# A Mamba-2 scan with a bilinear feed-forward on one core: blocks of all four batches at once, with four tokens a partition and 32-row tiles

## The chip, the cores and the metric

The kernel runs on one core of a Trainium2 chip. The metric is the device time of one execution in microseconds (us). The span that a profile shows is 1.7 us shorter than the device time of the same run (138.7 against 140.43). Runs of one kernel scatter; each is marked fast or slow (slow: over 1.5% above the fastest of its kernel). The profiled run of the kernel before, 140.43 us, is a slow one, so its first microseconds may differ from those of a fast run.

## The reference

The first half is a scan over 768 positions for 4 batches and 8 heads, with head dimension 32 and state dimension 16. The second half multiplies its output, as 3072 tokens of 256 columns, by two matrices of 256 x 1536, multiplies the two results with each other, and multiplies that by a matrix of 1536 x 256.

```python
for c in range(nc):                        # chunks of 32 in the reference
    cum = np.cumsum(la, axis=-1)
    L = np.exp(cum[:, :, :, None] - cum[:, :, None, :]) * causal
    M = np.einsum('bhin,bhjn->bhij', Cc, Bc) * L
    y_intra = np.einsum('bhij,bhjd->bhid', M, xc)
    y_inter = np.einsum('bhin,bhnd->bhid', Cc, state) * decay_to_i[:, :, :, None]
    y[:, :, sl] = y_intra + y_inter
    state = decay_full[:, :, None, None] * state + np.sum(Bx, axis=2)
# ...
x = attn_out.transpose(0, 2, 1, 3).reshape(B * S, H * D)
out = ((x @ w_a) * (x @ w_b)) @ w_out
```

## The kernel before

The kernel uses blocks of 128 positions, six of them. A block's work has five parts on TensorE: the transposes of scaled B and C, the **scores** (B times C), the **values** (masked scores times x, on top of the product of C with the carried state, here called inter), the **state** product, and the feed-forward: **units** (two products of X with columns of the first two weights) and **output** products. Two batches are worked on at a time, a "pair". A partition holds two consecutive positions of one batch, so that a contraction over positions runs over 64 partitions twice.

```python
def scores(p):                             # p is a pair of batches in a block
    BT, CT = st[p]["BT"], st[p]["CT"]
    for e in range(2):
        for r in range(2):
            for m in range(4):
                for bt in range(2):
                    rows = slice(32 * m, 32 * m + 32)
                    c0 = (e * 2 + r) * Q
                    nc.tensor.matmul(
                        SC[m][64 * bt : 64 * bt + 64, c0 : c0 + Q],
                        BT[rows, e, r, bt], CT[rows, bt],
                        start=True, stop=True, skip_group_check=True,
                        tile_position=(32 * m, 64 * bt),
                    )
# ... the steady loop:
for p in range(4, NP):
    scores(p)
    if p + 1 < NP:
        scale(p + 1)                       # GpSimd: next C, B and x times their factors
    if p + 2 < NP:
        load(p + 2)                        # two pairs ahead
    h = unit(p - 1, 0)
    mask(p, 0)                             # VectorE: scores times the causal mask
    h()
    mask(p, 1)
    mask(p, 2)
    h = unit(p - 1, 1)
    h()
    mask(p, 3)
    go((p - 1, 2))
    out_half(p - 2, 0)
    go((p - 1, 3))
    pull(p)
    pv(p)                                  # inter, values, state product
    state(p)
    if p + 1 < NP:
        transposes(p + 1)
    out_half(p - 2, 1)
    # ... (fb)
    go((p - 1, 4), (p - 1, 5))
```

Of the kernel before, what the change touches and what calls it, by code (L numbers as in the profile page):

```python
# [22 lines left out]
def kernel(  # L23
# [17 lines left out]
    Q = 128  # L41
    NBLK = S // Q
# [3 lines left out]
    NQ = NK // 2  # L46
    BH = nb * H
    NBP = nb // 2
    NP = NBP * NBLK
# [19 lines left out]
    causal = const.tile([128, 2, Q], f16, name="causal")  # L69
    sel = const.tile([BH, 2, NBP, H], f32, name="sel")  # L70
# [11 lines left out]
    X2T = big.tile([128, NP, 2, 2, Q], f16, name="X2T")  # L82
    U32 = big.tile([128, NP, 2, 2 * D], f32, name="U32")
    gU = big.tile([128, NP, 2, 2 * D], f32, name="gU")
    maskbd = big.tile([128, H, D], f16, name="maskbd")
    warm = big.tile([128, 512], f16, name="warm")
    scr = big.tile([128, 8], f32, name="scr")
    Pr = big.tile([BH, NBLK, Q], f32, name="Pr")
    rmid = big.tile([BH, NBLK], f32, name="rmid")
    selr = big.tile([BH, NBLK, 2, NBP * H], f32, name="selr")  # L90
    fB = big.tile([128, NBLK, 2, NBP, H], f32, name="fB")
    fC = big.tile([128, NBLK, 2, NBP, H], f32, name="fC")
# [5 lines left out]
    inp = ctx.enter_context(tc.tile_pool(name="inp", bufs=3))  # L98
    mid = ctx.enter_context(tc.tile_pool(name="mid", bufs=3))
    ffh = ctx.enter_context(tc.tile_pool(name="ffh", bufs=4))  # L100
# [3 lines left out]
    SC0 = ps4.tile([128, 2, 512], f32, name="SC0")  # L104
    SC1 = ps4.tile([128, 2, 512], f32, name="SC1")
    SC = [SC0[:, 0], SC0[:, 1], SC1[:, 0], SC1[:, 1]]
    TT = SC0[:, 0, :].bitcast(f16)

# [3 lines left out]
    pair_in = {}  # L112

    def tiles(p):
        Bn = inp.tile([128, H, 2, N], f32, name="bn", tag="bn")
        Cn = inp.tile([128, H, 2, N], f32, name="cn", tag="cn")
        Xn = inp.tile([128, H, 2, D], f32, name="xn", tag="xn")
        pair_in[p] = (Bn, Cn, Xn)

    def load1(eng, p, which, bt):  # L120
        blk, bp = divmod(p, NBP)
        src = (B, C, x)[which][2 * bp + bt, :, blk * Q : (blk + 1) * Q, :]
        return eng.dma_start(
            pair_in[p][which][64 * bt : 64 * bt + 64].rearrange("i h r n -> i h (r n)"),
            src.rearrange("h (i r) n -> i h (r n)", r=2),
        )

    def load(p, eng=None):
        tiles(p)
        return [load1(eng or nc.sync, p, w, bt) for w in range(3) for bt in range(2)]  # L130
# [3 lines left out]
    tiles(1)  # L134
    load1(nc.scalar, 0, 1, 0)
    load1(nc.sync, 0, 0, 0)
    load1(nc.scalar, 0, 1, 1)
    load1(nc.sync, 0, 0, 1)
    nc.scalar.preload_act_table_set("natural_log_exp_and_others")
    nc.scalar.dma_start(c32, p32_t.ap())  # L140
    load1(nc.sync, 0, 2, 0)
    load1(nc.sync, 0, 2, 1)
    for bt in range(2):
        load1(nc.scalar, 1, 1, bt)
        load1(nc.sync, 1, 0, bt)
    load1(nc.sync, 1, 2, 0)
    load1(nc.scalar, 1, 2, 1)
# [9 lines left out]
        pattern=[[-H, 2], [-2 * H, NBP], [-1, H]],  # L157
# [10 lines left out]
    def load_w(q3):  # L168
        for W, src in ((Wa, moe_w_a), (Wb, moe_w_b)):
            c = slice(q3 * KC, (q3 + 1) * KC)  # L170
            wd.append(nc.gpsimd.dma_start(W[:, :, c], src.rearrange("(f p) e -> p f e", p=128)[:, :, c]))

    load_w(0)
    nc.gpsimd.memset(causal, 1.0)
    for bt in range(2):
        v = causal[64 * bt : 64 * bt + 64]
        nc.gpsimd.affine_select(
            out=v, in_=v, compare_op=ALU.is_ge, fill=0.0, base=0, pattern=[[-1, 2], [1, Q]], channel_multiplier=-2
        )

    def warmup(n):
        w = psf.tile([128, 512], f32, name="wps", tag="ff")
        for _ in range(n):
            nc.tensor.matmul(w[:, 0:128], warm[:, 0:128], warm[:, 0:128], start=True, stop=True, skip_group_check=True)  # L184
# [6 lines left out]
    def sel_over_mid(lo, hi):  # L191
        nc.vector.reciprocal(rmid[:, lo:hi], Pr[:, lo:hi, 63])
        nc.vector.tensor_tensor(
            out=selr[:, lo:hi].rearrange("p k t c -> p k (t c)"),
            in0=sel.rearrange("p t b h -> p (t b h)").unsqueeze(1).broadcast_to((BH, hi - lo, 2 * NBP * H)),
            in1=rmid[:, lo:hi].unsqueeze(2).broadcast_to((BH, hi - lo, 2 * NBP * H)),
            op=ALU.mult,
        )

    def factors_mm(lo, hi):  # L200
        fps = psf.tile([128, 512], f32, name="fps", tag="ff")
        F = fps[:, 0 : (hi - lo) * 2 * NBP * H].rearrange("p (k r c) -> p k r c", k=hi - lo, r=2)
        for k in range(lo, hi):
            for r in range(2):
                for bt in range(2):
                    nc.tensor.matmul(
                        F[64 * bt : 64 * bt + 64, k - lo, r],
                        Pr[:, k].rearrange("p (i r) -> p r i", r=2)[:, r],
                        selr[:, k, bt],
                        start=True,  # L210
                        stop=True,
                        skip_group_check=True,
                        tile_position=(0, 64 * bt),
                    )
        return F.rearrange("p k r c -> p (k r c)")

    def flat(f, lo, hi):
        return f[:, lo:hi].rearrange("p k r b h -> p (k r b h)")
# [4 lines left out]
    def scale_x(p, eng):  # L223
        X16 = mid.tile([128, H, 2, D], f16, name="x16", tag="x16")
        xo, xi = X16.rearrange("p h r d -> p (h r d)"), pair_in[p][2].rearrange("p h r d -> p (h r d)")
        st.setdefault(p, {})["X16"] = X16
        if eng is nc.scalar:
            nc.scalar.mul(xo, xi, XS)
        else:
            eng.tensor_scalar(xo, xi, XS, None, ALU.mult)  # L230

    def scale_bc(p, which, eng):
        blk, bp = divmod(p, NBP)
        name, f = (("bm", fB), ("cm", fC))[which]
        m_ = mid.tile([128, 2, H, N], f16, name=name, tag=name)
        eng.tensor_tensor(  # L236
            out=m_,
            in0=pair_in[p][which].rearrange("p h r n -> p r h n"),
            in1=f[:, blk, :, bp].unsqueeze(3).broadcast_to((128, 2, H, N)),
            op=ALU.mult,  # L240
        )
        st.setdefault(p, {})[name] = m_

    def scale(p):
        scale_bc(p, 1, nc.gpsimd)
        scale_bc(p, 0, nc.gpsimd)
        scale_x(p, nc.gpsimd)

    def transposes(p, ps=None):
        s = st[p]  # L250
        TB, TC = (TT[:, 0:256], TT[:, 256:512]) if ps is None else [t_.bitcast(f16)[:, 0:256] for t_ in ps]
        for T_, src in ((TB, s["bm"]), (TC, s["cm"])):
            for r in range(2):
                nc.tensor.transpose(  # L254
                    T_[:, r * 128 : (r + 1) * 128], src[:, r].rearrange("p h n -> p (h n)"), ident
                )
        BT = mid.tile([128, 2, 2, 2, 64], f16, name="bt", tag="bt")
        CT = mid.tile([128, 2, Q], f16, name="ct", tag="ct")
        for e in range(2):
            o_ = BT[:, e].rearrange("p r t i -> p (r t i)")  # L260
            nc.scalar.activation(out=o_, in_=TB, func=AF.Copy, scale=par[:, e : e + 1])  # L261
        (nc.scalar.copy if ps is None else nc.vector.tensor_copy)(  # L262
            CT.rearrange("p t (i r) -> p r (t i)", r=2), TC.rearrange("p (r c) -> p r c", r=2)
        )
        s["BT"], s["CT"] = BT, CT

    def scores(p):
        BT, CT = st[p]["BT"], st[p]["CT"]
        for e in range(2):
            for r in range(2):  # L270
                for m in range(4):
                    for bt in range(2):
                        rows = slice(32 * m, 32 * m + 32)
                        c0 = (e * 2 + r) * Q
                        nc.tensor.matmul(  # L275
                            SC[m][64 * bt : 64 * bt + 64, c0 : c0 + Q],
                            BT[rows, e, r, bt],
                            CT[rows, bt],
                            start=True,
                            stop=True,  # L280
                            skip_group_check=True,
                            tile_position=(32 * m, 64 * bt),
                        )
        st[p]["T1"] = mid.tile([128, H, 2, Q], f16, name="t1", tag="t1")

    def mask_on_pool(p, m):
        tmp = mid.tile([128, 2, 2 * Q], f32, name="tmp", tag="tmp")
        nc.scalar.copy(tmp.rearrange("p e c -> p (e c)"), SC[m])
        nc.gpsimd.tensor_tensor(
# [76 lines left out]
    def state(p):  # L366
        blk, bp = divmod(p, NBP)
        if blk == NBLK - 1:
            return
# [263 lines left out]
```

## Time and profile before

| | before |
|---|---|
| device time, median of 3 runs | 139.27 us (137.64 to 140.62) |
| span of the profiled run | 138.7 us (a slow run) |
| TensorE busy | 125.3 us, 90% |
| steady pair of batches, start to start | 9.38 us, so 18.76 us for a block of four batches |
| matmuls of TensorE in the profile, each with a weight load | 1977 |

In the lines below and in the prediction, a timeline row gives start, duration, engine, line, operation, output and inputs, tile, shapes and the number of instructions in the group; brackets give the idle time before it and what released it. Matmuls overlap their predecessors (twelve output matmuls from 81.14 us are 1.47 us long, and the next group starts 1.31 us behind their start), so costs are read from start to start. Of the names, cn, bn and xn are a block's C, B and x as loaded; cm and bm are C and B times their factors, and ct and bt the same transposed; t is a masked score, sbd the carried state spread out for inter, gU the carried state times its decay; X2T is the scan's output as the feed-forward reads it, aps and bps are a unit's two products, and hk is what they give when multiplied. One caution: the row of the granted clock of the kernel before reads 9 in all slices, and yet four feed-forward matmuls took 0.85 us instead of 0.44 until 23.5 us. The matmuls decide, not the row.

### The profile page before, as it was taken

The page shows a single profiled execution, that of the slowest core. Times are in us where ns is not written, and L with a number is a line of the kernel's source. Part 1 is how long each engine was busy: PE and PEld are TensorE (multiplying, and loading weights), DVE is VectorE, ACT ScalarE, POOL GpSimd, SP SyncE. Part 2 cuts the span into 40 slices and gives each one's busy share as a digit, 9 for nine tenths or more (in the row PEclk, how much of TensorE's full clock was granted, in tenths as well). Part 3 has the DMA queues.
Part 4 walks back from the last instruction along what each step waited for, and adds up shares of the span by engine and source line. Part 5 has one row for each costly group of instructions (what it writes and reads, how often), then busy time and mean ns, then how long its engine had stood idle before and what let it go on. Part 6 is the DMA issues. An engine that isn't in the chain of part 4 may idle for free.

```text
span 138.7 us, 4777 instructions
## 1 busy us (share of the span) xinstructions
PE 125.3 (90%) x1977; PEld 107.2 (77%) x1977; DVE 88.3 (64%) x166; ACT 73.3 (53%) x148; POOL 52.2 (38%) x71
## 2 busy tenths in 40 slices
PE   6993499799698699999999999999999999999990
PEld 6783366788597578988888888888888888888870
DVE  2681358678557649498497594894975937935340
ACT  3132253585267165754856647548556486465520
POOL 7947431595040665470740923805408200000000
PEclk9999999999999999999999999999999999999999
DMA  3999999500126635355145261451541011020112
GB/s 76 144 209 202 193 190 196 107 19 2 43 64 128 118 115 100 94 107 124 38 73 128 63 126 43 93 132 45 83 116 43 0 38 43 8 70 2 38 38 76
DMA packets 44805, 12.22 MB, mean 88 GB/s; under 512 B 38576, under 2 KB 44752, under 8 KB 44784
## 3 DMA queue, kind: packets, MB, share of 16 engines
q1 hardware_dynamic: 38736, 9.02, 31.3%
q0 software_dynamic: 3216, 2.36, 11.7%
q10 hardware_dynamic: 2832, 0.54, 2.3%
q8 instruction: 15, 0.25, 0.7%
q14 instruction: 6, 0.05, 0.1%
HBM read 11.13 MB, written 3.15 MB: 103 GB/s over the span
## 4 chain that ended last, share of the span: by engine, by line
PE 77%; DMA 10%; DVE 4%; ACT 4%; issue 2%; SPq 1%; DVEq 0%; ACTq 0%
PE aps L405 24%; PE bps L405 21%; PE ops L422 20%; DMA bn<-in_B_dram 10%; PE SC L275 3%; PE SC L328 3%; PE SC L254 2%; DVE t L297 2%; DVE hk L415 2%; PE SC L314 2%; ACT asb L414 1%; PE SC L342 1%; ACT bt L261 1%; ACT ct L262 1%; ACT X2T L359 1%
## 5 line engine op out<-in xcount | busy, mean ns | idle before, releaser
L415 DVE TENSOR_TENSOR hk<-bps,asb 128x512 f16<-128x512 f32 x72 | 49.6, 689 | 25.9 <-ACT asb L414 23.5
L414 ACT COPY asb<-aps 128x512 f32<-128x512 f32 x72 | 42.2, 586 | 22.5 <-PE aps L405 21.0
L405 PE MATMUL aps<-X2T,Wa 128*128 128x256 f16 x288 | 45.1, 281 | 0.7 <-ACT X2T L359 0.7
L405 PE MATMUL bps<-X2T,Wb 128*128 128x256 f16 x288 | 44.6, 279 | 0.0
L422 PE MATMUL ops<-Wo,hk 128*128 128x256 f16 x288 | 35.2, 273 | 0.0
L405 PEld LDWEIGHTS <-Wa 128*128 128x128 f16 x288 | 27.8, 100 | 5.5 <-issue 0.9
L405 PEld LDWEIGHTS <-Wb 128*128 128x128 f16 x288 | 28.9, 100 | 4.0
L297 DVE TENSOR_TENSOR t<-SC,causal 128x512 f16<-128x512 f32 x47 | 30.9, 681 | 1.5 <-ACT osb L437 1.1
L422 PEld LDWEIGHTS <-hk 128*128 128x128 f16 x288 | 27.6, 98 | 3.2
L380 POOL TENSOR_TENSOR sbd<-U,maskbd 128x512 f16<-128x512 f32 x10 | 11.6, 1156 | 46.1 <-DVE U L376 37.0
L437 ACT ACTIVATE osb<-ops 128x256 f32<-128x256 f32 x23 | 8.8, 383 | 17.7 <-PE ops L422 17.7
L230 POOL TENSOR_SCALAR x<-xn 128x512 f16<-128x512 f32 x10 | 14.9, 1490 | 0.9 <-DMA xn<-in_x_dram 0.2
L261 ACT ACTIVATE bt<-SC,ch 128x256 f16<-128x256 f16 x22 | 9.2, 471 | 4.4 <-PE SC L254 4.3
L359 ACT ACTIVATE X2T<-SC 128x512 f16<-128x512 f32 x11 | 6.6, 597 | 8.5 <-PE SC L342 7.5
L236 POOL TENSOR_TENSOR cm<-cn,fC 128x256 f16<-128x256 f32 x12 | 7.6, 630 | 6.1 <-DMA cn<-in_C_dram 5.9
L376 DVE SCALAR_TENSOR_TENSOR U<-SC,G,gU 128x64 f32<-128x64 f32 x16 | 3.8, 279 | 7.0 <-ACT X2T L359 7.0
L254 PE MATMUL SC<-ident,bm 128*128 128x128 f16 x22 | 3.2, 231 | 4.1 <-DVE bm L236 4.1
L275 PE MATMUL SC<-ct,bt 32*64 32x128 f16 x384 | 5.6, 235 | 1.2 <-ACT ct L262 0.8
L184 PE MATMUL wps<-warm 128*128 128x128 f16 x47 | 5.6, 313 | 1.2 <-DVE warm L148 1.2
L275 PEld LDWEIGHTS <-bt 32*64 32x64 f16 x384 | 3.9, 112 | 3.4 <-issue 3.3
L236 POOL TENSOR_TENSOR bm<-bn,fB 128x256 f16<-128x256 f32 x10 | 6.2, 622 | 0.0
L314 PE MATMUL SC<-ct,sbd 128*128 128x128 f16 x40 | 3.9, 219 | 2.3 <-DVE t L297 2.3
(59 smaller groups left out, 69.3 us busy)
## 6 DMA issues: line engine op xcount, KB each, us to landing
xn<-in_x_dram SPq DMA_DIRECT2D x23, 128.0 KB, 3.3
out_dram<-osb SPq DMA_DIRECT2D x23, 128.0 KB, 1.8
bn<-in_B_dram SPq DMA_DIRECT2D x24, 64.0 KB, 2.8
cn<-in_C_dram SPq DMA_DIRECT2D x20, 64.0 KB, 2.7
Wa<-in_moe_w_a_dram POOLq DMA_DIRECT2D x3, 256.0 KB, 6.0
Wb<-in_moe_w_b_dram POOLq DMA_DIRECT2D x3, 256.0 KB, 7.6
Wo<-in_moe_w_out_dram POOLq DMA_DIRECT2D x1, 768.0 KB, 11.7
cn<-in_C_dram ACTq DMA_DIRECT2D x4, 64.0 KB, 4.9
```

The costliest lines, as they stand in the source:

```text
L230: eng.tensor_scalar(xo, xi, XS, None, ALU.mult)
L236: eng.tensor_tensor(out=m_, in0=pair_in[p][which].rearrange("p h r n -> p r h n"), in1=f[:, blk, :, bp].unsqueeze(3).broadcast_to((128, 2, ...
L261: nc.scalar.activation(out=o_, in_=TB, func=AF.Copy, scale=par[:, e : e + 1])
L275: nc.tensor.matmul(SC[m][64 * bt : 64 * bt + 64, c0 : c0 + Q], BT[rows, e, r, bt], CT[rows, bt], start=True, stop=True, skip_group_check=True,
L297: nc.vector.tensor_tensor(out=st[p]["T1"][:, 2 * m : 2 * m + 2].rearrange("p e r q -> p e (r q)"), in0=SC[m].rearrange("p (e c) -> p e c", ...
L359: nc.scalar.activation(out=X2T[:, p].rearrange("p u t q -> p t u q"), in_=SC1[:, :, 0:256].rearrange("p t (u q) -> p t u q", u=2), func=AF ...
L380: nc.gpsimd.tensor_tensor(out=Sbd.rearrange("p t (m c) -> p t m c", m=4), in0=U32[:, p].unsqueeze(2).broadcast_to((128, 2, 4, 2 * D)), in1 ...
L405: nc.tensor.matmul(ps[:, kk * 2 * Q : (kk + 1) * 2 * Q], W[:, f, k * 128 : (k + 1) * 128], X2T[:, p, f].rearrange("p t q -> p (t q)"), sta ...
L414: nc.scalar.copy(asb, a_ps)
L415: return lambda: nc.vector.tensor_tensor(out=s["hk"][:, 2 * k2 : 2 * k2 + 2, :].rearrange("p k q -> p (k q)"), in0=b_ps, in1=asb, op=ALU.mult)
L422: nc.tensor.matmul(o_ps[:, 0:d_model], hk[:, k, bt * Q : (bt + 1) * Q], Wo[:, k, :], start=(k == 0), stop=(k == NK - 1), skip_group_check= ...
L437: nc.scalar.activation(out=o_sb, in_=o_ps[:, 0:d_model], func=AF.Copy, scale=1.0 / (YS * YS))
```

## The change

The intent is to halve the number of rounds. All four batches of a block are worked on at once. A partition now holds four positions of one batch, so the contractions over positions have 32 rows in place of 64, done four times, and all small matmuls use 32x32 tiles. Feed-forward products take 512 columns. Since the scores of four batches would fill all eight of the kernel's accumulator tiles of 128x512 (four SC, and four that the feed-forward uses), they come in two halves by head parity, and half of the masks go over ScalarE and GpSimd. The input and middle buffers shrink from three to two. In the cut below, R and nb are 4; mask_on_pool lets ScalarE copy the scores and GpSimd multiply them; the first pv covers heads 0 to 3 and the second heads 4 to 7; prep_bc is GpSimd's multiplication of the next block's C and B; the list A holds a unit, an output product and three units.

```diff
-    inp = ctx.enter_context(tc.tile_pool(name="inp", bufs=3))
-    mid = ctx.enter_context(tc.tile_pool(name="mid", bufs=3))
+    inp = ctx.enter_context(tc.tile_pool(name="inp", bufs=2))
+    mid = ctx.enter_context(tc.tile_pool(name="mid", bufs=2))
# ...
+    def scores(t, e, banks):
# ...
+        for r in range(R):
+            for m in range(4):
+                for b in range(nb):
+                    rows = slice(32 * m, 32 * m + 32)
+                    nc.tensor.matmul(
+                        banks[m][32 * b : 32 * b + 32, r * Q : (r + 1) * Q],
+                        s["BT"][rows, e, r, b],
+                        s["CT"][rows, b],
# ...
+                        tile_position=(32 * m, 32 * b),
# ... values and state likewise: tile_position=(32 * b, 32 * g) and (32 * b, 32 * m)
+    def window(t, e, items):
+        scores(t, e, SC)
+        mask_on_pool(t, 6 + e, SC[3])
+        h = unit(*items[0][1:])
+        mask(t, e, SC[0])
+        h()
+        mask_on_pool(t, 4 + e, SC[2])
+        mask(t, 2 + e, SC[1])
+        run(items[1:])
# ...
+    def product(t):
+        inter(t)
+        pv(t, 0)
+        pv(t, 1)
+        if t < NG:
+            dstate(t)
# ... evacuations
+        window(t, 0, A)
+        if not last:
+            if t > 1:
+                load(t + 1)
+            prep_bc(t + 1)
+        window(t, 1, Bw)
+        if not last:
+            scale_x(t + 1, nc.gpsimd)
+        product(t)
# ...
```

## The prediction

Some of its prices were estimates of mine: 216 ns for a matmul of 512 columns in item 1, the rest of the 0.64 us of the scores in item 2 (0.15, from the 0.147 us between the start of the last score matmul, 78.367, and that of the unit behind it, 78.514, in the trace before), and 26.7 ns a row of factors in item 5 (half of the 53 ns measured for twice the columns). The +1.1 of item 2 has 0.09 a block taken off for inter, an estimate that no trace had shown. The "over 3 us" of rival (c) is a guess.

> **What bounds the kernel now.** I read the page's busy shares first, then the groups, the timeline of one steady round, the timeline of the start, and last the DMA issues.
>
> The page, part 1 and two lines of part 2:
>
> ```profile
> PE 125.3 (90%) x1977; PEld 107.2 (77%) x1977; DVE 88.3 (64%) x166; ACT 73.3 (53%) x148; POOL 52.2 (38%) x71
> ...
> PE   6993499799698699999999999999999999999990
> ...
> DMA  3999999500126635355145261451541011020112
> ```
>
> TensorE is the bound from a quarter of the span on; the holes are at the start, under a full DMA row. The groups on that path:
>
> ```profile
> L405 PE MATMUL aps<-X2T,Wa 128*128 128x256 f16 x288 | 45.1, 281 | 0.7 <-ACT X2T L359 0.7
> L422 PE MATMUL ops<-Wo,hk 128*128 128x256 f16 x288 | 35.2, 273 | 0.0
> L236 POOL TENSOR_TENSOR cm<-cn,fC 128x256 f16<-128x256 f32 x12 | 7.6, 630 | 6.1 <-DMA cn<-in_C_dram 5.9
> ```
>
> The timeline of a steady round, 78.15 to 87.53 us (start, duration, engine, what):
>
> ```profile
> 78.15 0.43 PE L275 MATMUL SC<-ct,bt 32*64 32x128 f16 x32
> 78.51 0.61 PE L405 MATMUL aps<-X2T,Wa 128*128 128x256 f16 x4
> 81.14 1.47 PE L422 MATMUL ops<-Wo,hk 128*128 128x256 f16 x12
> 83.33 0.39 PE L314 MATMUL SC<-ct,sbd 128*128 128x128 f16 x4
> 83.64 0.42 PE L328 MATMUL SC<-t,x 64*32 64x128 f16 x32
> 83.90 0.32 PE L342 MATMUL SC<-x,bm 64*32 64x64 f16 x16
> 84.15 0.29 PE L254 MATMUL SC<-ident,bm 128*128 128x128 f16 x2
> 84.27 0.28 PE L254 MATMUL SC<-ident,cm 128*128 128x128 f16 x2
> ...
> 86.74 1.28 SPq L123 DMA_DIRECT2D bn<-in_B_dram  x2
> 87.53 0.43 PE L275 MATMUL SC<-ct,bt 32*64 32x128 f16 x32
> ```
>
> Read differences of starts, since matmuls overlap. A pair of batches takes 9.38 us. Feed-forward: 12 groups of four matmuls at 0.4375 (5.25) and 24 output matmuls (2.61). The block work is the other 1.52: scores 0.36, inter 0.31, values 0.26, state 0.25, transposes 0.24, and 0.1 before the scores. TensorE has no real gap here. The last is the DMA: SyncE needs about 0.65 us to issue each load.
>
> At the start, four feed-forward matmuls take twice as long:
>
> ```profile
> 17.09 1.06 PE L405 MATMUL bps<-X2T,Wb 128*128 128x256 f16 x4
> ```
>
> and the chain of waits (start, duration, what) says what came before them:
>
> ```profile
> 5.07 10.20 DMA bn<-in_B_dram
> ...
> 15.36 0.44 DVE bm L236
> ```
>
> A start-to-start of 0.85 instead of 0.44 us lasts from 16.3 to 23.5. VectorE sat 4.5 us in front of that bm, whose load came at 15.3; the first feed-forward unit waited until 16.26.
>
> [...]here 256 columns take 109.4 ns[...], so I take 216 ns for 512.[...] from 83.644 the first 32 pairs of weight load and matmul start in bunches of eight, 3.4 ns apart in a bunch and 56 ns between bunches; the pairs behind them begin at 83.90[...] and then come every 8.2 ns.[...]
>
> **The change, part by part.** The order of instructions shows PE rows rising from 3859 to 5149: four tokens a partition means a contraction of 32 in place of 64, thus 32-row tiles and, for four batches, twice the small matmuls for scores, values and state.
>
> 1. Feed-forward: 48 matmuls of 512 columns a block in place of 96 of 256: 48 x 0.216 = 10.37 against 10.50 us. Saves 0.13 a block, 0.8 in six. The output product stays.
> 2. Small matmuls, per block of four batches[...]. Scores, two halves of 64 pairs: 0.23 for the first 32, 32 x 0.0082 = 0.26[...]: 0.64 each, 1.28 against 0.72. Values and state in one go, 128 + 64 pairs: 0.23 + 160 x 0.0082 + 0.12 = 1.66 against 2 x 0.51 = 1.02.[...] Sum +1.1 a block; less item 1, about +1.0. Five blocks: **+5 us**. If sixteen tiles ran in bunches of 56 ns all the way, this would be 0.
> 3. VectorE gives half of the masks to ScalarE (copy, 0.585) and GpSimd (1.15 each). Per block VectorE falls from some 15 to 13.5 us, ScalarE rises to about 13.3, GpSimd from 8.6 to 13.1 (cm and bm 1.25 each, x 3.0, sbd 2.3, gU 0.75, four masks 4.6). All are under 19.6, but GpSimd is now on TensorE's path and works in order.
> 4. Loads. Before, loads ran two pairs ahead. Now load(t+1) stands in SyncE's order behind the store of an output of the same window, and GpSimd multiplies the loaded C between the two halves of the masks. From the start of scores(t,0), t = 2 to 4: scores 0.7, one unit 0.86, output 1.31, copy and store to 3.9. Then four B and four C loads at about 0.6 (an estimate between 0.65 for 512 rows and 0.34 for the store's 128; these have 256), the last C begun at 8.1 and, with 2.5 to landing (median before: 2.7), there at 10.6. Then cm 11.85, bm 13.1, two masks to 15.4. TensorE wants the last mask at: two scores 1.4, eight units 6.9, two outputs 2.6, inter 0.53, first values 0.53, sum 12.0. **Wait of some 3.4 us in three blocks, 10 us**; even with 0.3 us an issue 1 us each stays. In block 1 load(2) waits for Wo, which I put at 27.5 (2.6 MB behind 14.5 us at the 200 GB/s that the page shows there); its last C is there at 34.5, the last mask at 39.3, and TensorE, with four units and one output since 30.2, is there at 37.4: about 2 to 2.8.
> 5. Start. Block 0 of all four batches comes first, before the weights, in runs of 256 and 512 bytes. The DMA records give 13.8 ns for 128 bytes and 19.1 for 256, so B and C cost a third less. But causal selects of 32 x 512 (four at about 0.68, from 0.42 for 256) hold GpSimd until 6.2, and cm is done at 7.8; scores at 9.4, 6.5 masks on VectorE (0.61 to 0.68) to 13.8, values, X2T at 15.4. The first unit starts at an effective 15.0 against 16.26, with all four batches. Against that, the factors of blocks 1 to 5 are now 160 rows in place of 40, with 32 columns of weights in place of 64. Before they took 2.1 us hidden under masks (8.7 to 10.8, 53 ns a row[...]); now 160 x 26.7 ns = 4.3 us stand in front of the third unit. Units 0 to 3 at half clock, G 0.6: units 0 to 7 and the transposes are done at about 30.2. Before, at 29.7, nine units and both pairs were done. **No gain from the start.**
>
> From 30.2: 64 units x 0.863 = 55.2, 24 outputs 31.3, blocks and transposes 19.4, waits 2.4 + 10.2 + 0.6 (X2T behind three copies), tail 3.6 as before. End at about 153. The same from the other side: 138.7, plus 5 and 13.2, less the 3.5 that TensorE now stands still between 24 and 50 us (0.7, twice 1.2, twice 0.4: the masks and copies of the first pairs). I lower it to **150.5** for what I may have placed too late: issue cost, the 8.2 ns, the factors.
>
> **Rivals.** (a) *GpSimd and the loads don't bind*: the waits of item 4 fall away, and the time is near 141. For it: GpSimd has 6 us of slack a block, and the loaded bytes are few. Against: it works in order, and no load can be there before its issue. (b) *The small tiles run at full width*: 16 at once, no extra on TensorE; with the waits 146 to 148, without them 136, faster by 2%. For it: bunches of eight start in 24 ns, so sixteen would fit in 56. Against: the state product, 8.2 ns a pair with half the columns. (c) *The half clock comes back*: waits of over 3 us may put TensorE back to half clock, adding 2 to 3 us each, 155 to 160. Before, a hole of 4 us ran at half clock on both sides, which settles nothing. (d) *The gap at the start was the real cost* and block 0 in one go ends it: 4 us gained. For it: 4 us of holes; against: the 4.3 us of factors.
>
> **Range and chances.** Item 2 is 0 to 6, item 4 4 to 16, item 5 -4 to +2, around a base of 138. The low ends together give about 139, the high ones over 160; 143 to 156 should hold it 8 times in 10. Faster by 2% needs (a) and (b) and (d): 5%. Within 2%: two of the three: 9%. Slower: 86%.
>
> **What would show it.** In the profile after: GpSimd's cm idle on the C load, several us in blocks 2 to 4, and TensorE idle before the second values product on a GpSimd mask (item 4). Start-to-start of 64 score matmuls near 0.64 and of values with state near 1.7 (item 2). Units of four matmuls at 0.863 (item 1). Factors of 4 us at half clock (item 5). Wrong it is if cm never waits, or if the pairs come every 3.5 ns; then the time lies near or under that of before.

## The result

| | before | after |
|---|---|---|
| device time, median of 4 runs on one chip | 139.19 us (137.64 to 140.62) | 163.13 us (162.33 to 164.07) |
| span of the profiled run | 138.7 us (slow run) | 160.6 us (fast run) |
| matmuls of TensorE in the profile, each with a weight load | 1977 | 2766 |
| TensorE busy | 125.3 us, 90% | 139.8 us, 87% |

The ratio is 1.177 (95% interval 1.164 to 1.189). Ratios are the mean time of one kernel's fast runs over that of the other's of the same rounds, so they are not quite the ratios of the medians. The change is slower by 24 us. The direction was foreseen; the size was not, and 163 lies above the range. (The prediction counts 3859 and 5149 rows of TensorE in the order of instructions; no view of a profile shows these. The profiles have 1977 and 2766 matmuls.)

The profile page after, its busy times, its row of the granted TensorE clock, and its groups:

```profile
PE 139.8 (87%) x2766; PEld 88.0 (55%) x2766; DVE 85.9 (54%) x156; ACT 77.6 (48%) x156; POOL 74.5 (46%) x70
...
PEclk9955555895999999879999779999789999999999
...
L386 PE MATMUL aps<-X2T,Wa 128*128 128x512 f16 x144 | 46.4, 404 | 0.1
...
L224 POOL TENSOR_TENSOR cm<-cn,fC 128x512 f16<-128x512 f32 (+1 forms) x6 | 6.5, 1079 | 29.4 <-DMA xn<-in_x_dram 16.5
L316 PE MATMUL SC<-t,x 32*32 32x128 f16 x768 | 9.3, 239 | 8.1 <-POOL t L286 7.8
```

Two things stand out. TensorE waits 7.8 us before the values for GpSimd's masks, and GpSimd stands idle before its multiplication of the next block's loaded C (cm) for 7.1, 5.9 and 6.9 us in blocks 2 to 4, each time until 0.1 to 0.6 us after the last C has landed: that is item 4 of the prediction. (The page's 16.5 us are block 2's 7.1 and the 9.4 before the C of block 1. An arrow names what ended nearest in time: x here, though cm reads only C.) And the clock row has dips that the kernel before did not show in its steady part: the start, and once in each block. The clock records give them exactly: half clock from 8.65 to 29.13 us, and then four times for 3.41 us, at 35.96, 66.68, 90.57 and 114.47. By the starts of the feed-forward matmuls in them, against those at full clock, the four cost 1.7, 0.7, 1.4 and 1.2 us, 4.9 in all.

Block 2 shows how the two hang together. TensorE's and GpSimd's timelines:

```profile
63.02 1.06 POOL L224 TENSOR_TENSOR cm<-cn,fC 128x512 f16<-128x512 f32 x1 [7.12 <-DMA xn<-in_x_dram]
63.60 0.77 PE L316 MATMUL SC<-t,x 32*32 32x128 f16 x68
64.04 1.05 POOL L224 TENSOR_TENSOR bm<-bn,fB 128x512 f16<-128x512 f32 x1
65.05 2.26 POOL L286 TENSOR_TENSOR t<-tmp,causal 128x512 f16<-128x512 f32 x2
67.37 0.81 PE L316 MATMUL SC<-t,x 32*32 32x128 f16 x60 [3.00 <-POOL t L286]
68.63 2.18 PE L401 MATMUL ops<-Wo,hk 128*128 128x256 f16 x12
```

The load comes late, GpSimd works in order (cm at 63.02, bm at 64.04, the masks at 65.05), its two masks end at 67.3, and the values that need them start then. The twelve output matmuls behind it take 2.0 us from start to start in place of 1.31, because TensorE runs at half clock from 66.68 to 70.09.

The start also went otherwise than I had worked out: the scores of block 1 begin at 35.31 us, where the prediction had TensorE ready for them at 30.2. TensorE's timeline there:

```profile
21.09 2.58 PE L190 MATMUL fps<-selr,Pr 32*32 32x8 f32 x160
...
31.07 0.40 PE L234 MATMUL SC<-ident,bm 128*128 128x128 f16 x4 [0.79 <-POOL bm L224]
...
35.31 0.73 PE L261 MATMUL SC<-ct,bt 32*32 32x128 f16 x64 [1.90 <-DVE ct L248]
```

### The profile page after: what moved, and what is told of

It reads as the page before. It is cut to its first block, busy times and chain, and to the rows that moved or that the text cites. A ratio compares the mean times of both kernels' runs of the same rounds, so it can differ in the third digit from the quotient of the medians.

```text
span 160.6 us, 6346 instructions
## 1 busy us (share of the span) xinstructions
PE 139.8 (87%) x2766; PEld 88.0 (55%) x2766; DVE 85.9 (54%) x156; ACT 77.6 (48%) x156; POOL 74.5 (46%) x70
## 3 DMA queue, kind: packets, MB, share of 16 engines
q0 software_dynamic: 3216, 2.36, 10.4%
## 4 chain that ended last, share of the span: by engine, by line
PE 50%; DMA 18%; SPq 14%; issue 5%; POOL 5%; DVE 3%; ACT 3%; POOLq 0%; DVEq 0%; ACTq 0%
PE ops L401 19%; SPq L116 13%; PE aps L386 11%; PE bps L386 11%; DMA xn<-in_x_dram 11%; DMA Wa<-in_moe_w_a_dram 4%; PE SC L261 3%; PE SC L316 3%; POOL t L286 2%; DMA cn<-in_C_dram 2%; DVE ct L248 2%; DMA bn<-in_B_dram 2%; PE SC L332 1%; PE SC L234 1%; ACT asb L395 1%
## 5 line engine op out<-in xcount | busy, mean ns | idle before, releaser
L396 DVE TENSOR_TENSOR hk<-bps,asb 128x512 f16<-128x512 f32 x72 | 49.8, 692 | 40.3 <-ACT asb L395 28.0
L395 ACT COPY asb<-aps 128x512 f32<-128x512 f32 x72 | 42.2, 587 | 15.7 <-PE aps L386 13.9
L386 PE MATMUL aps<-X2T,Wa 128*128 128x512 f16 x144 | 46.4, 404 | 0.1
L386 PE MATMUL bps<-X2T,Wb 128*128 128x512 f16 x144 | 45.9, 402 | 0.0
L286 POOL TENSOR_TENSOR t<-tmp,causal 128x512 f16<-128x512 f32 (+1 forms) x23 | 25.6, 1133 | 25.2 <-ACT tmp L285 25.2
L386 PEld LDWEIGHTS <-Wb 128*128 128x128 f16 x144 | 14.8, 102 | 19.1 <-issue 3.8
L224 POOL TENSOR_TENSOR cm<-cn,fC 128x512 f16<-128x512 f32 (+1 forms) x6 | 6.5, 1079 | 29.4 <-DMA xn<-in_x_dram 16.5
L386 PEld LDWEIGHTS <-Wa 128*128 128x128 f16 x144 | 13.5, 102 | 11.9 <-issue 2.7
L285 ACT COPY tmp<-SC 128x512 f32<-128x512 f32 x21 | 12.5, 594 | 10.7 <-PE SC L261 8.5
L316 PE MATMUL SC<-t,x 32*32 32x128 f16 x768 | 9.3, 239 | 8.1 <-POOL t L286 7.8
L274 DVE TENSOR_TENSOR t<-SC,causal 128x512 f16<-128x512 f32 x23 | 15.4, 675 | 0.7 <-PE SC L261 0.7
L346 ACT ACTIVATE X2T<-SC 128x256 f16<-128x256 f32 (+1 forms) x21 | 6.0, 356 | 19.3 <-PE SC L332 16.5
L216 POOL TENSOR_SCALAR x<-xn 128x1024 f16<-128x1024 f32 x5 | 13.9, 2772 | 1.5 <-DMA xn<-in_x_dram 1.2
L361 POOL TENSOR_TENSOR sbd<-U,maskbd 128x1024 f16<-128x1024 f32 x5 | 10.6, 2127 | 0.8 <-DVE U L355 0.5
## 6 DMA issues: line engine op xcount, KB each, us to landing
Wo<-in_moe_w_out_dram POOLq DMA_DIRECT2D x1, 768.0 KB, 13.7
```

What stands on the lines that cost most here:

```text
L216: eng.tensor_scalar(xo, xi, XS, None, ALU.mult)
L274: nc.vector.tensor_tensor(out=st[t]["T1"][:, h, r].rearrange("p r q -> p (r q)"), in0=bank[:, c], in1=causal[:, r].rearrange("p r q -> p ( ...
L285: nc.scalar.copy(tmp[:, c], bank[:, c])
L286: nc.gpsimd.tensor_tensor(out=st[t]["T1"][:, h, r].rearrange("p r q -> p (r q)"), in0=tmp[:, c], in1=causal[:, r].rearrange("p r q -> p (r ...
L316: nc.tensor.matmul(PY[b][32 * g : 32 * g + 32, u * Q : (u + 1) * Q], s["X16"][k, h, r, :], s["T1"][k, h, r, :], start=(t == 0 and u == 0 a ...
L361: nc.gpsimd.tensor_tensor(out=Sbd.rearrange("p b (m c) -> p b m c", m=4), in0=U32[:, t].unsqueeze(2).broadcast_to((128, nb, 4, 2 * D)), in ...
```

## The experiments

Twelve kernels were run. Each call used one chip and its own runs of the kernel before: medians 137.74, 139.10 and 138.67 us. Ratios are therefore compared, not times of different calls. The theory at the outset had three parts: late loads that hold GpSimd and its masks (with a half clock behind each wait), small matmuls bound by the supply of instructions, and a slow start.

### e1: the loads ahead of the first half

```diff
+        if not last and t > 1:
+            load(t + 1)
         window(t, 0, A)
         if not last:
-            if t > 1:
-                load(t + 1)
             prep_bc(t + 1)
```

> The loads of block t+1 are issued before the first half of block t, ahead of the store, nothing else. Theory (late loads hold GpSimd's cm, cm holds the second half of the masks, the masks hold TensorE): the waits of 3.0, 1.8 and 2.8 us before the second values product and the half clock behind each go, together 11 us: 152 us, 1.095 of the kernel before. Rival (GpSimd has too much work in all, the loads only show it): the wait comes back in front of the masks or of sbd, 159 us or more.

Measured: 153.93 us, ratio 1.115 (1.105 to 1.125), correct; some 2 us over what I expected. The waits of the values on GpSimd's masks are gone in blocks 2 to 4. In block 2 all 128 run in one go:

```profile
65.11 1.26 PE L316 MATMUL SC<-t,x 32*32 32x128 f16 x128
```

So the late loads are shown as one part of their cause that they can't do without; e2 tests the other, the order on GpSimd. But the profiled run, a slow one of 157.86 us, has gaps that no wait explains, 2.20 us in block 2 and 1.54 us in block 3. The next run has them in a fast profile.

### e2: GpSimd's multiplications after the second half's masks

```diff
         window(t, 0, A)
         if not last:
             if t > 1:
                 load(t + 1)
-            prep_bc(t + 1)
         window(t, 1, Bw)
         if not last:
+            prep_bc(t + 1)
```

> The loads stay late; GpSimd's cm and bm of block t+1 come after both halves of the masks instead of between them. Theory (order on GpSimd, not the bytes): the same 11 us, 152 us, though the loads land as late as before. Rival (the transfers themselves are too slow): the wait moves to the transposes of block t+1, 159 us or more.

Measured: 154.32 us in the one fast run (the profiled one), and 157.51, 158.83 and 159.84 in three that count as slow. The computed ratio, 1.150, rests on those three, so I don't use it: what e2 gains in time rests on one run. The mask waits are gone here too, though the loads are issued in the same late place. In their place stands a gap "issue", which is time in which TensorE waited for nothing that the profile shows. TensorE's timeline in block 2:

```profile
61.34 1.26 PE L316 MATMUL SC<-t,x 32*32 32x128 f16 x128
62.40 0.59 PE L332 MATMUL SC<-x,bm 32*32 32x64 f16 x48
65.54 0.29 PE L332 MATMUL SC<-x,bm 32*32 32x64 f16 x16 [2.55 <-issue]
65.75 2.74 PE L401 MATMUL ops<-Wo,hk 128*128 128x256 f16 x12
```

The places of these gaps are a lead. Counted in matmuls of the trace, the gaps of e2 stand before matmul 1374 and 1758, 384 apart, three times 128. Those of e1 stand before 351, 479, 1374 and 1758: from the first, 128, 1023 and 1407, which is one, eight and eleven times 128 within a record or two. So a new theory, which no trace shows directly: the gaps belong to places in TensorE's stream of instructions, and TensorE runs out of instructions where many small matmuls pass quickly.

### e3: spare matmuls in the wait

```diff
         pv(t, 0)
+        if 1 < t < NG:
+            for _ in range(30):
+                nc.tensor.matmul(SC[0][:, 320:448], warm, warm, start=True, stop=True, skip_group_check=True)
         pv(t, 1)
```

> 30 spare matmuls (1.7 us, into unused columns) between the two values products of blocks 2 to 4, where TensorE waits; nothing else. Theory (each wait also costs 3.4 us of half clock): the three half clock stretches after the waits go, the outputs behind them take 1.31 us instead of 2.0 to 2.7: 3 us less, 160 us. Rival (the clock falls for another reason, or 1.7 us of work in a wait of 1.8 to 3.0 is too little): the granted clock stays at 0.9 and the time at 163 or a little over.

Measured: 158.88 us, ratio 1.150 (1.141 to 1.160), against 1.177 for the changed kernel: some 3.6 us less, for thirty more matmuls a block. The result was wrong (relative error 0.055): the spare matmuls went into a bank to whose other columns the values are still being added. That is my mistake; whether it is the cause is not shown. Its instructions are those of the changed kernel plus the spare ones, and they wait for the same things, so I use its times; as a version it is no use. The twelve output matmuls behind the wait of block 2 take 1.32 us again:

```profile
68.04 1.48 PE L401 MATMUL ops<-Wo,hk 128*128 128x256 f16 x12
69.36 0.59 PE L386 MATMUL aps<-X2T,Wa 128*128 128x512 f16 x2
```

Its clock row has no dips in blocks 2 to 4:

```profile
PEclk9955576995999999999999999999999999999999
```

From the scores of block 2 to the end of the span it takes 3.1 us less than the changed kernel (105.4 against 108.5), about the 3.3 us that the half clock cost there. So the half clock behind each wait is shown as a cost of its own.

### e4: block 1's loads not held behind the weights

```diff
-    n0 = load(1)
-    tc.add_manual_dep(n0[0].ins, wd[2].ins.name, AFTER, reason="weights first")
+    load(1)
```

> Block 1's loads do not wait for the third weight transfer. Theory (the start lost 5 us against my estimate, mostly because these loads shared the DMA engines with the late weights): cm of block 1 runs at 24 instead of 28.9 us, the transposes wait no longer, scores of block 1 begin 2 to 4 us earlier: 160 us. Rival (the weights are the shorter side): the first units wait for them instead, 163 us or more.

Measured: 166.86 us, ratio 1.205 (1.191 to 1.219). The scores of block 1 came at 38.13 us, later than 35.31. Part of the theory held: cm ran at 27.06 in place of 28.94 us, and TensorE's wait before the transposes was gone. But TensorE stood still in the first block's values, again without a wait, while loads filled the DMA (9 tenths busy in that slice of the page):

```profile
18.99 0.82 PE L316 MATMUL SC<-t,x 32*32 32x128 f16 x61 [2.42 <-issue]
```

That gap stands before matmul 351. A second one of 0.72 us stands before matmul 479, in front of the factors that cm needs. So the loads' share in the late start is not settled by this run.

### e5: every score matmul in two of 64 columns

```diff
+                    for c in (0, 64):
                         nc.tensor.matmul(
-                            banks[m][32 * b : 32 * b + 32, r * Q : (r + 1) * Q],
+                            banks[m][32 * b : 32 * b + 32, r * Q + c : r * Q + c + 64],
                             s["BT"][rows, e, r, b],
-                            s["CT"][rows, b],
+                            s["CT"][rows, b, c : c + 64],
# ...
```

> The changed kernel with every score matmul split into two of 64 columns: the same products and the same tiles, twice the instructions (128 pairs a half in place of 64). Theory A, the small matmuls are bound by the supply of instructions (8.3 ns a pair once 32 pairs are through): from the first score matmul to the following unit 1.19 us in place of 0.66, some 5 us more in five blocks, 168 us[...]. Theory B, they are bound by the columns that pass through a tile[...]: 0.66 us as before and 163 us.

Measured: 177.64 us in a single run. The changed kernel has 0.66 us from the first score matmul to the next unit:

```profile
52.10 0.73 PE L261 MATMUL SC<-ct,bt 32*32 32x128 f16 x64 [0.50 <-DVE ct L248]
52.76 0.60 PE L386 MATMUL aps<-X2T,Wa 128*128 128x512 f16 x2
```

e5 has 1.18 us:

```profile
62.63 1.24 PE L262 MATMUL SC<-ct,bt 32*32 32x64 f16 x128 [0.48 <-DVE ct L248]
63.81 0.60 PE L387 MATMUL aps<-X2T,Wa 128*128 128x512 f16 x2
```

The same products and the same tiles, with twice the instructions, take almost twice as long: the small matmuls are bound by the number of instructions, not by columns or by what a change of tile shape costs. That it is their supply, as theory A had it, and not a fixed cost of each pair is not tested alone; for it speaks that the first 32 pairs of a run start within 0.12 us and only the later ones every 8.3 ns. The time rose by much more than its 5 us. The scores of block 1 began only at 41.45 us, and gaps "issue" stood before matmuls 351, 479, 607 and 862 (1.2 to 2.4 us from start to start), once more whole multiples of 128 apart within a record or two.

### e6: the stream moved by 40 matmuls

The loads stand as in e1, and three groups of warm-up matmuls are left out.

```diff
-    warmup(28, w0)
...
-    warmup(10, w0)
...
-    warmup(2, w0)
```

> The kernel of e1 (loads ahead of the first half) with 40 warm-up matmuls less at the start, so that everything behind stands 40 matmuls earlier in TensorE's stream. Theory A, TensorE runs out of instructions: in e1 its stalls without any wait stood before matmuls 351, 479, 1374 and 1758 of the trace, apart by whole multiples of 128 matmuls[...], and none stood in block 4. The boundaries keep their places in the stream, so against the work they move: block 2's falls 96 matmuls into its values and state in place of 56 and 184, and its stall of 2.2 us vanishes; block 3's fall at 48 and 176 and its stall grows from 1.5 to about 2.2 us; block 4's fall at 0 and 128 and it gets a stall of 1 to 2 us, which e1 did not have. Theory B, the stall belongs to the state product itself or to its operands: blocks 2 and 3 stall as in e1, 2.2 and 1.5 us, block 4 not.

Measured: 160.97 us in a single run, with a start that suffered most (gaps of 2.07, 1.82 and 3.28 us before matmuls 223, 351 and 479). Block 2 ran without a gap; block 3 stalled before the same matmul 1758 of the stream, which is now its 41st state matmul, 176 into its small matmuls, as computed:

```profile
90.90 0.52 PE L332 MATMUL SC<-x,bm 32*32 32x64 f16 x40
93.70 0.32 PE L332 MATMUL SC<-x,bm 32*32 32x64 f16 x24 [2.29 <-issue]
```

The gap that I expected in block 4 did not come. There one of these places fell just at the first inter matmul, and TensorE went through without a pause (units at 112.16 and 112.59 us, inter at 113.03, values at 113.57); why is not shown. So two of three expectations held, and the stall belongs to a place in the instruction stream and not to the state product. That what runs between two such places decides whether TensorE stalls is my reading; how instructions come to TensorE is not shown.

### e7: the transposed C of block 1 first

```diff
     tcp = turn(1)
-    U(0, 6)
     evac_c(1, tcp)
+    U(0, 6)
```

> The changed kernel with one move: the first evacuation of the transposed C (block 1) stands ahead of feed-forward unit 6 on VectorE, not behind its product. Theory, the start lost 2.3 us in that order: VectorE copies ct at 31.7 instead of 33.9, the scores of block 1 start at about 33.4 instead of 35.3, TensorE's gap of 2.28 us shrinks to under 0.5, and the time falls by 1.9 us, ratio to before about 1.163. Rival, the time lost there is made up by a later wait in block 1 for GpSimd's masks (its loads are issued from 31.8 whatever VectorE does): the time stays within 0.7 us of the changed kernel's.

Measured: 164.37 us, ratio 1.187 (1.175 to 1.199, so within the noise of the changed kernel's 1.177), no gain at all. The scores of block 1 did start earlier, at 31.24 us, but the scores of block 2 at 52.17 as before (52.10). The rival held: TensorE waited further on, for GpSimd's masks in block 1.

```profile
40.48 2.26 POOL L286 TENSOR_TENSOR t<-tmp,causal 128x512 f16<-128x512 f32 x2
42.80 0.81 PE L316 MATMUL SC<-t,x 32*32 32x128 f16 x60 [2.15 <-POOL t L286]
```

TensorE's clock took a part too: in block 1, e7's clock row reads 5 in two slices (40.3 to 48.4 us), the changed kernel's in one (36.1 to 40.2; its record has 3.41 us at half clock). GpSimd had been busy since 30.28 us almost without a pause: x of block 1, the state spread out, the decayed state, two masks, block 2's C and B, two masks. That chain starts when x of block 1 lands.

### e10: two pieces off that chain

e7, with block 1's x scaled on VectorE and block 2's C and B multiplied after the masks of block 1.

```diff
-    scale_x(1, nc.gpsimd)
...
     U(0, 7)
+    scale_x(1, nc.vector)
...
-            prep_bc(t + 1)
+            if t > 1:
+                prep_bc(t + 1)
         window(t, 1, Bw)
         if not last:
+            if t == 1:
+                prep_bc(t + 1)
```

> e7 (the transposed C of block 1 evacuated first) with two more moves, both off GpSimd's chain in block 1: the scaling of x for block 1 goes to VectorE, and GpSimd multiplies block 2's C and B after the second half's masks of block 1 and not before. Theory, the end of block 1 was set by GpSimd's chain from the landing of block 1's x (in e7 30.28 to 42.74 us without a pause: 2.8 + 2.1 + 0.6 + 2.3 + 2.1 + 2.3), which is why e7 gained nothing: the values of block 1 run without the wait of 2.37 us at 42.8, the scores of block 2 start at about 48 us instead of 52.1, and the time falls by 3.5 to 4.5 us against the changed kernel, ratio about 1.145. Rival, the output weights or block 2's loads are next: the scores of block 2 do not start before 51 us and the time stays above 161.

Measured: 158.71 us, ratio 1.146 (1.130 to 1.161). The scores of block 2 start at 48.23 us, against 52.10 in the changed kernel:

```profile
48.23 0.73 PE L261 MATMUL SC<-ct,bt 32*32 32x128 f16 x64 [0.76 <-DVE ct L248]
```

Both were foretold (48, and 1.145), so the end of block 1 was set by GpSimd's chain; that no half clock falls into block 1 any more is part of the gain. What each of the two moves gives is not separated. In blocks 2 to 4 the waits and their half clock are all still there (3.11, 2.10 and 3.16 us).

### e9: the small matmuls broken up

e1, with an output product and a unit between the two values products, and two outputs before the state product, taken from the places before and after.

```diff
         inter(t)
         pv(t, 0)
+        run(fill[0])
         pv(t, 1)
-        if t < NG:
-            dstate(t)
         # ... evacuations
+        run(fill[1])
+        if t < NG:
+            dstate(t)
# ... the lists of work around it, shorter by what fill holds
```

> e1 with the small matmuls of each block broken up: an output product and a unit (16 matmuls, 2.2 us) between the first and second values product, two output products (24 matmuls, 2.6 us) between values and state; the same work, moved from before and after. Theory A, instruction supply: 128 matmuls now never take under about 3 us except in block 1, the stalls of 2.2 and 1.5 us in blocks 2 and 3 vanish, no half clock follows, the mask waits stay at nothing, and the time is about 149 (e1: 153.9), ratio 1.08 to 1.09. If 3 us of the rest were also due to the burst's own rate (8.3 ns a pair) it would show as a lower steady period; I expect the period of a block without stall at 19.9 to 20.2 us, a little over e1's for two more changes of tile mode. Theory B, the stall is due to load traffic or to the state product: stalls of 1.5 us or more remain before the state product.

Measured: 156.34 us, ratio 1.132 (1.120 to 1.145), so 7 us over what I expected and not better than e1 (the two intervals just overlap). The mechanism held: no gap "issue" and no half clock in blocks 2 to 4. The price was elsewhere. With the units moved, VectorE's copy of the transposed C came late, TensorE waited 0.84 us for it in each of these blocks, and they followed each other every 21.29 us.

### e11: all that helped, together

e10, e2 for the later blocks, e9's breaking up, and the copy of the transposed C ahead of the next unit in every block.

> All that helped, together: e10's start, for blocks 2 to 4 the multiplication of the next C and B after the masks as in e2, the small matmuls broken up by units and output products as in e9, and the transposed C evacuated ahead of the next unit in every block. If the changed kernel's excess of 24 us is what I read (waits 7.8 and half clock after them 3.5; start and block 1 some 4; small matmuls 5; the rest exposed order), this removes all but the small matmuls: the scores of block 2 start at 48 us, blocks follow every 20.3 us without half clock, and the time is 148 to 150 us, ratio 1.065 to 1.08. If it stays above 153, a term is missing from my account.

Measured: 148.30 us, ratio 1.077 (1.066 to 1.088), inside what I expected. The scores of block 2 start at 48.03, the next three blocks follow after 20.37, 20.70 and 20.37 us, and there is no half clock behind the start. The clock row of the page:

```profile
PEclk9999996899999999999999999999999999999998
```

and the values of block 2, with large matmuls between them (timeline):

```profile
57.36 0.73 PE L316 MATMUL SC<-t,x 32*32 32x128 f16 x64
58.02 1.49 PE L401 MATMUL ops<-Wo,hk 128*128 128x256 f16 x12
...
60.30 0.73 PE L316 MATMUL SC<-t,x 32*32 32x128 f16 x64
60.97 2.79 PE L401 MATMUL ops<-Wo,hk 128*128 128x256 f16 x24
```

### e8 and e12: the kernel before with its start reordered

These were tries for a version that beats both. e8 evacuates the first pair's X before VectorE waits for the second pair's B, makes the decay sums earlier, and runs two units in TensorE's hole from 11.5 to 15.8 us:

```diff
     scale_bc(1, 1, nc.gpsimd)
-    scale_bc(1, 0, nc.vector)
...
     pv(0, [bank("py0"), bank("py1")])
-    transposes(1)
...
     state(0)
+    go((0, 0))
+    h = unit(0, 1)
+    scale_bc(1, 0, nc.vector)
     h()
+    transposes(1)
+    go((0, 2))
     scores(1)
```

> The kernel before with another order at the start, for a version that may beat both: VectorE evacuates the first pair's X before it waits for the B of the second pair, the decay sums are made earlier, and the feed-forward units 0 and 1 of the first pair fill TensorE's hole of 4 us from 11.5 to 15.8. Expected if that hole was on the path: units start at about 12.5 instead of 16.3, the second pair's values at about 22.5 instead of 24.1, and the time falls by 1.5 to 2.5 us, ratio 0.982 to 0.990. Rival, the path at the start is the masks of the second pair and weights still landing: less than 0.7 us.

Measured: 140.88 us, ratio 1.020 (1.011 to 1.029). The second pair's values did come earlier, at 22.73 us in place of 24.07. But TensorE had a gap of 3.02 us between starts before them, and the units behind ran at half clock for 3.41 us, 0.81 us for four matmuls:

```profile
22.73 0.42 PE L328 MATMUL SC<-t,x 64*32 64x128 f16 x32 [2.75 <-DVE t L297]
...
24.03 1.01 PE L405 MATMUL aps<-X2T,Wa 128*128 128x256 f16 x4 [0.73 <-ACT X2T L359]
24.84 1.06 PE L405 MATMUL bps<-X2T,Wb 128*128 128x256 f16 x4
```

The third pair's scores stood at 31.48 us against 31.39 in the profile before, which is of a slow run. e12 fills that hole with 48 spare matmuls:

```diff
     mask(1, 3)
+    warmup(48)
     pv(1)
```

> e8 (the kernel before with its start reordered) with 48 idle matmuls that fill TensorE's hole of 3.02 us before the second pair's values. In e8 this hole was followed by 3.41 us at half clock, which took back the 1.3 us won by then. Theory: without the hole the clock stays full, the units after it run at 0.44 us for four matmuls in place of 0.85, the scores of the third pair start at 29.9 instead of 31.5 us, and the time is 1.0 to 1.7 us under e8's, about 1% within the kernel before. Rival: the masks of the third pair wait for GpSimd or the loads anyway, and the time is e8's.

Measured: 139.68 us, ratio 1.015 (1.007 to 1.022). The half clock is gone, and the third pair's scores start at 30.88. TensorE then waits 1.73 us for the masks of that pair (34.20 to 35.93). So the next wait takes part of what is won. Whether the start bounds the kernel before is not settled by this: e12 is 1.5% slower than its fast runs, and none of these was profiled. No version that I ran beats the kernel before.

## Why the prediction was wrong

By its own steps:

- **Item 1 (units) and item 2 (small matmuls): right.** A unit's two groups of 512 columns took 0.865 us, foretold 0.863. 64 score pairs took 0.66 us, foretold 0.64; values with state 1.70, foretold 1.66. In the trace after, 32 pairs start within 0.12 us, the next one 0.24 us after the first (foretold 0.23), and the rest every 8.3 ns (foretold 8.2), for 128 columns and for 64 alike. e5 shows that the number of instructions is what costs. A block without stalls takes 19.93 us (e2, block 4: scores at 95.31 and 115.24) against 18.76, so +1.2 a block where +1.0 was foretold.
- **Item 3: right**: GpSimd is on TensorE's path, and no engine is full. From the scores of one block to those of the next, in blocks 2 to 4, GpSimd was busy for 11.5 to 12.0 us (foretold 13.1), ScalarE 12.4 to 12.7 (13.3) and VectorE 13.3 to 13.5 (13.5). VectorE's "some 15" before was read too high: the trace has 13.7 to 13.9.
- **Item 4 (late loads): right mechanism, the sum 4.8 us too large.** Foretold were 10.2 us in blocks 2 to 4 and 2.4 in block 1; the values waited 7.8 us. In block 2 nearly every step came as worked out, counted from its scores: the first load issued after 3.9 us (foretold 3.9), the last C landed after 10.4 (10.6), the masks done after 15.2 (15.4), TensorE there after 12.0 (12.0). Block 3's wait was only 1.8 us, and block 1's did not come because TensorE itself was late; in e7, where it is early, 2.15 us of it appear. e1 and e2 remove the waits, each by one of their two conditions: loads issued behind a store, and GpSimd's order.
- **Rival (c), half clock behind the waits: dismissed, and true. This is the first step that failed.** "Before, a hole of 4 us ran at half clock on both sides, which settles nothing" was correct, and I then put it at zero. The runs showed four stretches of 3.41 us, which cost 0.7 to 1.7 us each and 4.9 us in all, where the rival had put 2 to 3 us each; and half clock followed a wait of 1.8 us too (block 3), not only the "waits of over 3 us" of the rival. e3 gives back about 3.6 us by filling three waits partly.
- **Item 5 (start): the second step that failed.** "No gain from the start ... done at about 30.2" was 5.1 us too early. The terms in the trace: the first unit started at 17.26 in place of an effective 15.0; half clock held until 29.13, through unit 4, one unit more than foretold (+0.7); TensorE waited 0.8 us for block 1's B and 1.9 us for the copy of the transposed C; the transposes themselves (0.5) are missing in the sum; the factors took 2.5 us in place of 4.3 (-1.8). These add up to 4.4 of the 5.1; the rest is small delays between units. But e7 shows that not all of it was on the path. GpSimd's chain from the landing of block 1's x set the end of block 1, and only e10, which shortens the chain, gains: 4.3 us of 139 (ratio 1.177 to 1.146).
- **The lowering from 153 to 150.5: wrong.** It was taken for things perhaps placed too late, while the missing terms all lay on the other side.

With the failed terms put in, the sum comes near: 153 foretold, 5.1 for the start, 4.9 for half clock, 1.0 for five blocks of +1.2 in place of +1.0, less 4.8 for smaller waits, is 159.2 for a span of 160.6. The other 1.4 us stay open.

What the experiments add is where the excess sits when taken off step by step. From ratio 1.177 to 1.146 (some 4 us) goes with GpSimd's chain in block 1 and the half clock there. From 1.146 to 1.077 (some 9.5 us) goes with the mask waits, their half clock and the order that avoids the gaps "issue". What is left, 1.077 or some 10.7 us, is mostly the small matmuls: blocks of 20.4 to 20.7 us against 18.76. Some 1.2 us of that difference is the number of instructions (the block without stalls above); that the other 0.4 to 0.8 comes from the extra changes of tile shape which the breaking up needs is likely, but no run separates it. A remainder of 2 to 3 us, by subtraction, is not taken apart either.

One thing I did not foresee: **a wait hid another.** In the changed kernel the mask wait of block 2 (64.14 to 67.37) stood between two of those places in the stream: matmul 1246 is among the 68 values ahead of it, matmul 1374 among the state matmuls behind it. When e1 and e2 took the wait away, 2.75 and 1.86 us (e2) of it came back as "issue". A block of four batches now has 8 inter, 128 values and 64 state matmuls in a row, 400 instructions in 2.2 us where no gap falls into them (e6, block 4: 113.03 to 115.27). In block 2 of e2 they took 5.0 us (60.80 to 65.75). The one fast run of e2 and its three slow ones differ by 3.2 to 5.5 us in a kernel whose work is fixed; that gaps of varying length cause this is a guess, for no slow run of e2 was profiled.

## What to carry to other kernels

Smaller tiles at equal work mean more instructions, and a small matmul costs its place in the instruction stream (here 8.3 ns a pair behind the first 32, with 128 columns and with 64): count instructions, and spread long runs of them between large matmuls. Price each expected wait of TensorE at its own length plus the half clock that may follow (here 3.41 us of it, which cost 0.7 to 1.7). When a wait vanishes and the time stays, look at what then stands in the same place: here a late mask hid a stall of 2.75 us for which no wait is shown (e2, block 2), and an early start was eaten by a chain on GpSimd.

## What else the traces show

- TensorE had gaps of 0.7 to 3.3 us for which no wait is shown, whole multiples of 128 matmuls apart within a record or two (before matmuls 223, 351, 479, 607, 862, 1374 and 1758 of various kernels). Quick small matmuls are not the only place: at the start, where the DMA is 9 and 5 tenths busy on the page, one came though the 128 matmuls ahead of it had taken 5.7 us (e6, from matmul 351 at 19.91 to the gap that begins at 25.64).
- After the start, the half clock of the changed kernel comes in stretches of 3.41 us (at 35.96, 66.68, 90.57 and 114.47). A gap between starts of 1.98 us was followed by one (after, block 3), but one of 2.28 us was not (e2, before the scores of block 1), nor one of 1.86 us (e2, block 3), nor one of 2.93 us (e5, block 3). So the length of a gap alone does not tell, and the runs give no threshold.
- With 32x32 tiles, the first 32 pairs of a run start within 0.12 us, but the pairs behind them every 8.3 ns over long runs (after, scores at 52.10). This second rate sets what small tiles cost.
- VectorE took 1.28 us (1.25 to 1.29 in six copies) to copy 128x512 f16 elements to places four apart, and 0.41 us in one copy of 128x256 to places two apart: 1.6 times as long for each element. The cause is not tested.
